# Exponent arguments from one stationary tile of 128 rows, with the hi and lo parts of both logarithms stacked

## The chip, the cores and the metric

The kernel runs on one core of one Trainium2 chip. Five engines work from queues of their own: TensorE (PE, matrix products into PSUM), VectorE (DVE), ScalarE (ACT, functions from tables), GpSimd (POOL) and SyncE (SP, which issues most of the transfers). The metric is the device time of one execution in microseconds.

## The reference

`x` is 2048 positions by 640 channels. A layer norm, scaled and shifted by vectors computed from a condition `c`, feeds a state space convolution; its output, gated, is added to `x`; a second norm feeds a gated feed-forward block of width 1728, which is added too.

```python
dt = exp(log_dt)[:, None]; logdA = dt * (A_re + 1j * A_im)
P = exp(logdA[:, :, None] * l[None, None, :])            # 640 x 128 x 2048
K = einsum("dn,dnl,dn->dl", Cc, P, dt * Bc).real          # one filter of 2048 taps a channel
y = irfft(rfft(u, 2L) * rfft(K, 2L))[:L] + u * Dskip      # causal convolution
out = (silu(h @ w1) * (h @ w3)) @ w2
```

The change concerns the filter `K` alone. The position is split as l = 64 a + b, with a below 32 and b below 64, so that the filter of a channel is a product of a slow table (over a) and a fast table (over b) summed over the 128 states n. A table entry is exp(decay) times a cosine or a sine. The magnitude of C B dt^2 goes into the slow table's exponent as half its logarithm squared.

## The kernel before, in words

Channels are worked in 40 steps of 16 (step k; 8 steps make one of five chunks of 128 channels). For each step:

- PA (`exp_fast`, lines 444 to 454) makes the fast exponents on PE, 128 states by 16 channels by 64 values of b, into a PSUM tile `pa`. XA (`fast`) takes their Exp on ACT into the table `A`.
- PQ (`exp_slow`, lines 455 to 465) and XQ (`slow`) do the same for 32 values of a, in `pq`.
- PH makes phases on POOL, in integers; AB, CO and SI (`absph`, `cosine`, `sine`, lines 496 to 507) turn them into a cosine and a sine on ACT.
- E1, E2, A1, A2 multiply exponentials and trigonometric tables on DVE; kg multiplies the tables on PE into the filter, K scales it on DVE, pt takes the first stage of its transform on PE, uk copies it out on ACT.

Ten steps behind, the convolution works on chunks already transformed: st (second stage of the transform, line 590), kc, T, Y (products), iv (inverse, line 632), zt (copy and store).

The exponents are products of a logarithm with a step length. TensorE rounds its fp32r operands, so each logarithm is split into a rounded part hi and the rest lo. `polar` (lines 237 to 291) makes both logarithms with states on the partitions: the decay `are * dt` in `lt[:, 0]` and the magnitude `q + ld` in `lt[:, 1]`. It turns them by PE with one transpose per chunk and logarithm (line 283), and splits what comes out on ACT (line 285, the rounded copy) and DVE (line 286, the difference). That gives four tiles `lah`, `lal`, `lmh`, `lml` with 128 channels of a chunk on the partitions, in four groups r of 32 rows. `polar` runs for chunk 0 in the head of the kernel, and for chunks 1 to 4 spread over the first loop.

The moving operands are `r2` (fast) and `r1` (slow): a 32 x 32 unit matrix (`selx`), each one multiplied by the step lengths (`stepx`), so that each of 32 rows yields its own channel's exponents. `sel`, half the unit matrix, adds half the magnitude. A half step (rr) is 8 channels in one group of 32 rows. Fast: two matmuls (hi and lo) for each of two half steps, 4. Slow: four (hi and lo of the decay on `r1`, hi and lo of the magnitude on `sel`) for each of two, 8. All of them use 32 rows of the array.

The order of work: the head and the first loop (`for tk in range(LAG)`) are ordered by the planner except what is marked to keep its order; ACT always keeps it. There, exponents are made for two steps at once (`exps`), in two PSUM buffers A and B, which `u_stage1` and `polar` use as well. Behind it come ten rounds of four steps, whose order is the list `ROUND` word by word (line 841): all engines keep it. In the rounds pa and pq have the single buffer B. In rounds 2 to 6 the rest of the conditioning vectors is computed in five late pieces, each called right behind a word of the list (lines 853 to 857): `late_load` (a transfer), `late_sums` (PE, line 299), `late_part` (DVE), `late_cols` (PE, lines 366 and 370), `late_out` (DVE). The feed-forward block stands behind the rounds, with its matmuls at lines 1059 to 1110 and 1258, all recorded at line 102.

Of the kernel before, what the change touches and what calls it, by code (L numbers as in the profile page):

```python
# [17 lines left out]
P = 128  # L18
L = 2048
D = 640  # L20
# [17 lines left out]
def consts():  # L38
# [32 lines left out]
    stepx = np.concatenate([np.arange(NB), 64 * np.arange(NA)])[None].repeat(P, 0)  # L71
# [36 lines left out]
def tile_kernel(ctx: ExitStack, tc: tile.TileContext, a):  # L108
# [50 lines left out]
    hp = kp.tile([P, 1], F32, name="hp")  # L159
    V.memset(hp, math.pi / 2)  # L160
# [13 lines left out]
    lah = once([P, KD, P], F32R, "lah")  # L174
    lal = once([P, KD, P], F32R, "lal")
    lmh = once([P, KD, P], F32R, "lmh")
    lml = once([P, KD, P], F32R, "lml")
    r2 = once([P, NA, NB], F32R, "r2")
    r1 = once([P, NA, NA], F32R, "r1")
    sel = once([P, NA], F32R, "sel")  # L180
# [5 lines left out]
    lt = pm_.tile([P, 2, D - DC], F32, name="lt")  # L186
# [50 lines left out]
    def polar(cs, E):  # L237
# [37 lines left out]
        rows = lambda v: v[:, :nk * P].rearrange("n (k r p j) -> n k r p j", k=nk, p=4, r=4)  # L275
        for k in range(nk):
            E.tensor_tensor(rows(lt[:, 0])[:, k], nat(are)[:, k], nat(dtc)[:, k], op=OP.mult)
        for k in range(nk):
            V.tensor_tensor(rows(lt[:, 1])[:, k], nat(q)[:, k], nat(ld)[:, k], op=OP.add)
        for i, (hi, lo) in enumerate(((lah, lal), (lmh, lml))):  # L280
            pT = psS.tile([P, 2, 512], F32, name="pT", tag="AB"[i], bufs=1)
            for k in range(nk):
                PE.transpose(pT[:, 0, k * P:(k + 1) * P], lt[:, i, k * P:(k + 1) * P], ident)
            pv = pT[:, 0, :nk * P].rearrange("p (k n) -> p k n", k=nk)
            acopy(hi[:, k0:k0 + nk], pv)
            V.tensor_tensor(lo[:, k0:k0 + nk], pv, hi[:, k0:k0 + nk].bitcast(F32), op=OP.subtract)
# [151 lines left out]
    def exp_rows(s):  # L438
        return s // SPC, slice((s % SPC) // 2 * 8, (s % SPC) // 2 * 8 + 8), [
            (rr, slice((2 * (s % 2) + rr) * 32, (2 * (s % 2) + rr) * 32 + 32)) for rr in range(2)]  # L440

    pA, pQ = {}, {}

    def exp_fast(steps):

        for s in steps:
            pA[s] = psS.tile([P, 2, 512], F32, name="pa", tag="AB"[s % 2] if not in_order[0] else "B", bufs=1)
        for w, st in ((lah, True), (lal, False)):
            for s in steps:
                ch, js, rows = exp_rows(s)  # L450
# [50 lines left out]
    def cosine(s):  # L501
        act(cs[s], cs[s], AF.Sin, scale=-2 * math.pi / TURN, bias=hp)
# [946 lines left out]
```

## Time and profile before

| | |
|---|---|
| median of 3 runs | 1009.01 us (1006.81 to 2960.16) |
| profiled execution | 1006.52 us, span 1004.4 us |
| granted TensorE clock, mean | 0.95 |
| busy: PE, DVE, ACT, POOL | 922.5, 730.2, 543.3, 349.5 us |
| line 452 (`pa`), PE busy | 33.6 us |
| line 464 (`pq`), PE busy | 29.4 us |

The page of the profile gives busy times of the whole span; views of the trace give groups of instructions by line, the chain of work that ended last, instructions in order of time (start, length, engine, operation, "output<-input", and in brackets the idle time before it with what ended it), and busy times by stretch. A row in order of time may merge neighbours of one kind (x2, x16). Busy times of PE overlap, since matmuls are pipelined.

### The profile page before, as it was taken

To read this page: it belongs to the slowest core of one execution; us is meant where nothing else is said; L and a number is where in the kernel's file an instruction comes from. 1 tells how busy PE (TensorE), PEld (TensorE's weight loads), DVE (VectorE), ACT (ScalarE), POOL (GpSimd) and SP (SyncE) were. 2 spreads that over 40 slices of the span, in tenths; PEclk is the share of its full clock that TensorE was granted. 3 is DMA by queue.
4 is the path that set the end of the run, shared out by engine and by line. 5 is a ranking of instruction groups with operands and counts; after the bars stand their busy time and mean duration, and the time that the engine had idled before them with its cause. 6 is when DMAs were issued, how large, how long until landed. Compare 5 with 4: busy or idle time off the path is not lost.

```text
span 1004.4 us, 20629 instructions
## 1 busy us (share of the span) xinstructions
PE 922.5 (92%) x8214; PEld 689.2 (69%) x8214; DVE 730.2 (73%) x1227; ACT 543.3 (54%) x793; POOL 349.5 (35%) x330
## 2 busy tenths in 40 slices
PE   5898779999989888789999999989989999999998
PEld 2535456666666666467888888766768888888786
DVE  4598887888888885677666675687696666676765
ACT  3658687988889953255433332344643333333332
POOL 1543353434444611314222233444342222224441
PEclk9855779999999999999999999999999999999999
DMA  9462393666665689592221213969231111123352
GB/s 268 170 234 80 135 237 106 160 179 181 189 174 139 182 211 265 183 278 77 70 61 55 56 37 104 254 204 282 86 128 56 54 53 53 53 81 103 92 199 76
DMA packets 103571, 140.74 MB, mean 140 GB/s; under 512 B 20564, under 2 KB 62676, under 8 KB 103476
## 3 DMA queue, kind: packets, MB, share of 16 engines
q1 hardware_dynamic: 92692, 113.60, 39.4%
q10 hardware_dynamic: 8480, 18.09, 6.1%
q0 software_dynamic: 2304, 7.74, 2.4%
q8 instruction: 64, 1.05, 0.4%
q14 instruction: 31, 0.25, 0.1%
HBM read 107.94 MB, written 31.46 MB: 139 GB/s over the span
## 4 chain that ended last, share of the span: by engine, by line
PE 62%; ACT 14%; DVE 10%; DMA 7%; issue 3%; POOL 3%; SPq 1%; ACTq 0%; DVEq 0%; POOLq 0%
PE ps L102 43%; PE p L590 4%; ACT cs L135 3%; ACT A L135 3%; PE pa L452 2%; ACT ph L135 2%; PE pz L632 2%; PE pk L541 2%; PE pq L464 2%; DMA zs<-zt 2%; DMA A<-zs 2%; ACT L135 2%; PE pt L559 1%; PE pu L426 1%; DMA rw<-in_w_dram 1%
## 5 line engine op out<-in xcount | busy, mean ns | idle before, releaser
L102 DVE TENSOR_TENSOR s<-ps,s 128x512 f32<-128x512 f32 x138 | 94.8, 688 | 77.0 <-PE ps L102 76.3
L492 POOL TENSOR_TENSOR ph<-thi,iota 128x1024 int32<-128x1024 int32 x40 | 85.4, 2135 | 170.2 <-DVE A L528 79.1
L102 DVE TENSOR_TENSOR gl<-rw,gh 128x640 fp32r<-128x640 f32 x87 | 84.2, 968 | 62.4 <-ACT gh L102 59.4
L102 ACT CAST gh<-rw 128x640 fp32r<-128x640 f32 x87 | 63.2, 727 | 115.4 <-PE ps L102 79.6
L102 POOL TENSOR_TENSOR rw<-rw,gbr 128x512 f32<-128x512 f32 x56 | 82.4, 1478 | 104.4 <-DMA rw<-in_w_dram 90.1
L102 POOL TENSOR_TENSOR S<-rw 128x256 f32<-128x256 f32 x46 | 35.7, 778 | 176.2 <-DVE S0l L102 159.1
L590 PE MATMUL p<-uk,s 128*64 128x256 f32 x640 | 79.2, 390 | 15.3 <-PE pa L452 5.6
L102 PE MATMUL ps<-xA,gh 128*128 128x512 f32 x280 | 89.0, 396 | 0.7 <-DVE h L102 0.4
L102 PE MATMUL ps<-gh,uh 128*128 128x512 f32 x224 | 89.3, 399 | 0.0
L102 PE MATMUL ps<-gl,uh 128*128 128x512 f32 x224 | 88.8, 397 | 0.0
L102 PE MATMUL ps<-gh,ul 128*128 128x512 f32 x208 | 82.5, 397 | 0.0
L590 PEld LDWEIGHTS p<-uk,s 128*64 128x64 f32 x640 | 45.2, 138 | 40.6 <-PE pa L452 8.4
L102 PEld LDWEIGHTS ps<-xA,gh 128*128 128x128 f32 x280 | 53.0, 191 | 14.0 <-ACT xA L102 0.9
L102 PE MATMUL ps<-xA,gl 128*128 128x512 f32 x140 | 55.3, 395 | 0.3 <-DVE gl L102 0.3
L135 ACT ACTIVATE A<-pa 128x1024 f32<-128x1024 f32 x40 | 40.4, 1024 | 25.4 <-PE pa L452 23.9
L517 DVE TENSOR_TENSOR E<-A,cs 128x1024 f32<-128x1024 f32 x40 | 52.3, 1307 | 2.5 <-ACT cs L135 1.8
L559 PE MATMUL pt<-s,K 128*64 128x128 f32 x640 | 48.7, 297 | 4.9 <-ACT uk L138 4.9
L524 DVE TENSOR_TENSOR A<-A,ph 128x1024 f32<-128x1024 f32 x40 | 50.3, 1256 | 0.0
L102 PEld LDWEIGHTS ps<-gl,uh 128*128 128x128 f32 x224 | 43.2, 193 | 9.5
L102 PEld LDWEIGHTS ps<-gh,uh 128*128 128x128 f32 x224 | 43.2, 193 | 9.1
L632 PEld LDWEIGHTS pz<-Y,i 64*128 64x128 f32 x640 | 38.5, 187 | 15.5 <-issue 13.1
L632 PE MATMUL pz<-Y,i 64*128 64x128 f32 x640 | 44.5, 283 | 4.5 <-issue 3.5
(244 smaller groups left out, 2366.7 us busy)
## 6 DMA issues: line engine op xcount, KB each, us to landing
rw<-in_w_dram ACTq DMA_DIRECT2D x44, 320.0 KB
us<-u SPq DMA_DIRECT2D x16, 640.0 KB
s<-in_s_dram SPq DMA_DIRECT2D x40, 256.0 KB
i<-in_i_dram SPq DMA_DIRECT2D x40, 256.0 KB
rw<-in_wg_dram SPq DMA_DIRECT2D x31, 320.0 KB
rw<-in_wu_dram SPq DMA_DIRECT2D x28, 320.0 KB
uk<-us SPq DMA_DIRECT2D x32, 256.0 KB
zs<-zt SPq DMA_DIRECT2D x32, 256.0 KB
```

The source lines that it names most:

```text
L102: ins = fn(*args, **kw)
L135: return tc.keep_in_program_order(S.activation(*args, **kw))
L426: PE.matmul(pu[h][hh * 64:hh * 64 + 64, q, :320], s1r[r], x[r, hh * 320:hh * 320 + 320], start=not (one and h == 0), stop=True, tile_posit ...
L452: keep(PE.matmul(pA[s][:, rr, :], w[r, ch, :], r2[r, js, :].rearrange("p j b -> p (j b)"), start=st, stop=not st, tile_position=(r.start, 0)))
L464: keep(PE.matmul(pQ[s][:, rr, :256], w[r, ch, :], rv, start=(i == 0), stop=(i == 3), tile_position=(r.start, 0)))
L492: hold(G.tensor_tensor(p, bc(thi[:, sl], 2, NPH), bc(iota, 1, SD), op=OP.mult))
L517: keep(V.tensor_tensor(EC[s][:, :, 1:3, :], AA[s][:, :, 1:3, :], mid(cs[s]), op=OP.mult))
L524: keep(V.tensor_tensor(A[:, :, 1:3, :], A[:, :, 1:3, :], mid(ph[s]), op=OP.mult))
L541: keep(PE.matmul(pk[dq * 32:dq * 32 + 32, g, :], x[:, g * 4 + dq, 1, :], x[:, g * 4 + dq, 0:3:2, :], start=(st == 0), stop=(st == 1), tile ...
L559: keep(PE.matmul(pt[c * 64:c * 64 + 64, g, :], kk[:, g, :], s1[:, c, :], start=True, stop=True, tile_position=(0, c * 64)))
L590: keep(PE.matmul(p2[par * 64:par * 64 + 64, pi, c, :], s2[:, pi * 2 + par, c * 64:c * 64 + 64], uk[:, 0:kn + 1:kn, f, :], start=True, stop ...
L632: ins = keep(PE.matmul(pz[:, par, (g % 2) * 2 + pi, :], i1[r, pi, c, :], Y[r, pi, c, :], start=(c == 0), stop=(c == 1), tile_position=(par ...
```

## The change

The four tiles become one, `lx`, with 128 rows for each group of 32 channels: 32 rows each of decay hi, magnitude hi, decay lo, magnitude lo. `polar` lays both logarithms side by side in `lt`, multiplies each such block by the unit matrix twice, into the upper and the lower 64 partitions of PSUM, rounds all of it, and replaces the lower half by the difference. The step lengths in `stepx` have the matching rows: for the magnitude 0 (fast) and 0.5 (slow). One matmul over 128 rows then yields a half step: 2 for the fast, 2 for the slow exponents of a step. `sel` goes. Beside that, the cosine's bias becomes a number in place of the tile `hp`, and the late pieces become words of the round (LS, LP, LC, LO), each standing one word earlier than it ran before; the load stands ahead of the round's first word.

```diff
-    stepx = np.concatenate([np.arange(NB), 64 * np.arange(NA)])[None].repeat(P, 0)
+    stepx = np.tile(np.concatenate([np.arange(NB), 64.0 * np.arange(NA)]), (4, NA, 1)).reshape(P, NB + NA)
+    stepx[P // 4:P // 2] = stepx[3 * P // 4:] = np.repeat((0, 0.5), (NB, NA))
...
-    lah = once([P, KD, P], F32R, "lah")
-    lal = once([P, KD, P], F32R, "lal")
-    lmh = once([P, KD, P], F32R, "lmh")
-    lml = once([P, KD, P], F32R, "lml")
+    lx = once([P, KD, 4, P], F32R, "lx")
...
-        for i, (hi, lo) in enumerate(((lah, lal), (lmh, lml))):
-            pT = psS.tile([P, 2, 512], F32, name="pT", tag="AB"[i], bufs=1)
-            for k in range(nk):
-                PE.transpose(pT[:, 0, k * P:(k + 1) * P], lt[:, i, k * P:(k + 1) * P], ident)
-            pv = pT[:, 0, :nk * P].rearrange("p (k n) -> p k n", k=nk)
-            acopy(hi[:, k0:k0 + nk], pv)
-            V.tensor_tensor(lo[:, k0:k0 + nk], pv, hi[:, k0:k0 + nk].bitcast(F32), op=OP.subtract)
+        low = slice(P // 2, P)
+        for k in range(0, nk, 2):
+            n = min(2, nk - k)
+            pT = psS.tile([P, 2, 512], F32, name="pT", tag="AB"[k // 2], bufs=1)
+            for i in range(n):
+                for r in range(4):
+                    for h in range(2):
+                        PE.matmul(pT[h * 64:h * 64 + 64, i, r * P:(r + 1) * P],
+                                  lt[:, k + i, r].rearrange("n i c -> n (i c)"), ident,
+                                  start=True, stop=True, tile_position=(0, h * 64))
+            to = lx[:, k0 + k:k0 + k + n].rearrange("p k r n -> p k (r n)")
+            acopy(to, pT[:, :n])
+            V.tensor_tensor(to[low], pT[low, :n], to[low].bitcast(F32), op=OP.subtract)
...
+    def exponents(to, steps, table, n):
+        for s in steps:
+            ps = to[s] = psS.tile([P, 2, 512], F32, name="pa", tag="AB"[s % 2] if not in_order[0] else "B", bufs=1)
+            js = slice((s % SPC) // 2 * 8, (s % SPC) // 2 * 8 + 8)
+            for rr in range(2):
+                keep(PE.matmul(ps[:, rr, :8 * n], lx[:, s // SPC, 2 * (s % 2) + rr, :],
+                               table[:, js, :].rearrange("p j b -> p (j b)"), start=True, stop=True))
...
-        act(cs[s], cs[s], AF.Sin, scale=-2 * math.pi / TURN, bias=hp)
+        act(cs[s], cs[s], AF.Sin, scale=-2 * math.pi / TURN, bias=math.pi / 2)
...
-        "PA+6 E2+3 pt+2 XA+6 A2+3 E2+4 kc+4 PQ+6 uk+2 PH+7 T+4 kg+3 XQ+6 AB+6 PA+7 K+3 iv+2 XA+7 AB+7 "
-        "Y+4 PQ+7 A1+4 st+5 XQ+7 A2+4 PH+8 kg+4 CO+5 iv+3 kc+5 K+4 CO+6 T+5 pt+3 zt+3 Y+5 uk+3 E1+5 "
+        "PA+6 E2+3 pt+2 XA+6 A2+3 E2+4 kc+4 PQ+6 uk+2 PH+7 T+4 kg+3 XQ+6 AB+6 LS+4 PA+7 K+3 iv+2 XA+7 "
+        "AB+7 LP+4 Y+4 PQ+7 A1+4 LC+4 st+5 XQ+7 LO+4 A2+4 PH+8 kg+4 CO+5 iv+3 kc+5 K+4 CO+6 T+5 pt+3 "
```

46 lines of the change are left out of this document (13 added, 33 removed), and 2 rows, old and new, of the table ROUND.

## The prediction

> **What bounds the kernel now.** I read the page's span first, then where the exponents stand (the view of line 452), then the table of busy time by stretch, since one mean covers very unlike stages.
>
> ```profile
> span 1004.4 us, 20629 instructions
> ...
> L452 PE MATMUL pa<-r,lal x80: 382/392/792, 24.1 to 348.5; 32*128 32x512 f32 x80
> ...
> core 0: us, PE busy (x) PEld busy (x) DVE busy (x) ACT busy (x) POOL busy (x), PEclk, DMA share, GB/s
> 100.00:135.00 35.00, 28.06 (x430) 15.93 (x426) 31.37 (x53) 24.23 (x30) 13.76 (x11) 0.68 0.41 154
> 195.00:225.00 30.00, 27.41 (x514) 19.78 (x510) 24.82 (x42) 26.34 (x33) 12.96 (x8) 1.00 0.64 175
> ```
>
> The last fast exponent starts at 348.5 us; no edit reaches behind that but four cosines, so the other 650 us only start earlier or later. Steps 0 to 3 lie in the head, 4 to 11 in the first loop (to 135 us, TensorE well under its full clock: granted 0.68), 12 to 39 in seven written-out rounds. In a round no engine is full: PE 27.4 of 30 us, ACT 26.3, DVE 24.8, and they wait for each other in turn. The ACT queue of a round shows where:
>
> ```profile
> 217.84 1.02 ACT L135 ACTIVATE A<-pa 128x1024 f32<-128x1024 f32 x1
> ...
> 232.44 0.60 ACT L135 ACTIVATE A<-pq 128x512 f32<-128x512 f32 x1 [1.19 <-PE pq L464]
> 233.06 1.28 ACT L135 ACT_TABLE_LOAD   x1
> ...
> 237.48 1.01 ACT L138 COPY zt<-pz 128x1024 f32<-128x1024 f32 x1 [0.46 <-PE pz L632]
> ...
> 239.95 1.14 ACT L135 ACTIVATE cs<-cs,hp 128x1024 f32<-128x1024 f32 x1
> 240.98 1.05 ACT L135 ACTIVATE ph<-ph 128x1024 f32<-128x1024 int32 x1
> 241.93 1.05 ACT L135 ACTIVATE cs<-ph 128x1024 f32<-128x1024 int32 x1
> ...
> 248.18 1.02 ACT L135 ACTIVATE A<-pa 128x1024 f32<-128x1024 f32 x1
> ...
> 251.70 1.02 ACT L135 ACTIVATE A<-pa 128x1024 f32<-128x1024 f32 x1 [1.08 <-PE pa L452]
> ```
>
> A round lasts 248.18 - 217.84 = 30.34 us. Its first half (Exp) is ping-pong: pa and pq share one PSUM buffer, so ACT waits for PE (1.08 and 1.19 us in these rows) and PE for ACT. Its second half (Sin, from the table load at 233.06) has ACT back to back but for 0.46 us.
>
> **The fast exponents (pa).** Four matmuls become two. In PE's queue:
>
> ```profile
> 249.25 0.39 PE L464 MATMUL pq<-r,lah 32*128 32x256 f32 x2 [0.58 <-ACT A L135]
> 249.48 0.28 PE L464 MATMUL pq<-r,lal 32*128 32x256 f32 x2
> 249.60 0.27 PE L464 MATMUL pq<-sel,lmh 32*128 32x256 f32 x2
> ...
> 249.91 1.09 PE L559 MATMUL pt<-s,K 128*64 128x128 f32 x16
> ...
> 255.30 0.50 PE L452 MATMUL pa<-r,lah 32*128 32x512 f32 x2
> 255.64 0.39 PE L452 MATMUL pa<-r,lal 32*128 32x512 f32 x2
> 255.96 0.88 PE L559 MATMUL pt<-s,K 128*64 128x128 f32 x12
> ...
> 132.51 0.57 PE L452 MATMUL pa<-r,lah 32*128 32x512 f32 x4
> 132.92 0.39 PE L452 MATMUL pa<-r,lal 32*128 32x512 f32 x4
> ...
> 467.18 141.99 PE ps L102 x625
> ```
>
> The two of a pair sit in different groups of 32 rows and run side by side: a pair takes 255.64 - 255.30 = 0.34 and then 0.32 us, and at 132.51 four of them take 0.41. So four instructions are two passes of 512 columns, and the new two are also two passes. A full-array pass is priced by the MLP: 141.99 / 625 = 0.227 us. Two of them with the weight load before the first (0.34 - 0.227 = 0.11) take 0.57 to 0.66 us against 0.66. I take nothing, and keep 0.21 (2 x 0.227 against 0.66) as the other end. The Trainium skill, "TensorE: Matmul & The Clock Gate", Part 3, says this of the form removed: a matmul on 32 rows lasts as long as one on 128, the gain being that several run at once; the trace agrees (0.41 us for four). The Trainium skill's same page, "Back-to-back issue gap", gives about 131 ns for a 512-column matmul in a stream, by which two would cost 0.26 us, an estimate; the 0.227 us here speaks against it, and the sum does not use it.
>
> **The slow exponents (pq).** Here eight become two: 249.91 - 249.25 = 0.66 us for four pairs, the first 0.23, the second 0.12, the last two 0.31 with the change of shape behind them. Two passes go, at 0.12: 0.24 us a step, both in PE's time and in ACT's wait. Ends: 0 (the two that stay lose their side-by-side loads) and 0.43 (all but the first).
>
> **The cosine's bias.** A number takes the place of a tile.
>
> ```profile
> L135 ACT ACTIVATE cs<-cs,hp 128x1024 f32<-128x1024 f32 x40 | 46.0, 1149 | 0.4
> ...
> L135 ACT ACTIVATE ph<-ph 128x1024 f32<-128x1024 int32 x40 | 41.4, 1050 | 0.0
> ```
>
> Sine, which has no such tile, is 99 ns shorter; in the queue above, starts lie 1.03 us apart behind a cosine and 0.95 behind a sine. I take 0.09 us each, 0.36 a round (0 if the number is put into a tile after all).
>
> **The late pieces moved** (rounds 2 to 6). LS now stands ahead of PA+7, LC ahead of st+5, LP ahead of Y+4, LO ahead of A2+4; the load of xw is issued ahead of E1+2 in place of behind it, and since E1+2 issues no DMA, SP's queue keeps its order; POOL has no part in any of it.
>
> ```profile
> 229.18 1.48 PE L299 MATMUL pm<-xw,sc 128*32 128x384 f32 x10
> ...
> 234.48 0.83 PE L366 MATMUL pm<-one,xw 128*128 128x1 f32 x6
> ...
> 231.79 0.42 DVE L614 TENSOR_TENSOR Y<-T,p 128x256 f32<-128x256 f32 x1 [2.51 <-PE pz L632]
> ```
>
> LP falls into the 2.51 us in which DVE waits ahead of Y. LO is a new wait of DVE ahead of A2+4: it waits for LC, behind it are A2+4 and then kg+4 on PE; since A1+4 (1.2 us) stands before it, I cost it at nothing, and at LC's 0.83 if A1+4 were not there.
>
> **One round walked through**, counted from its first Exp at 217.84. PQ+4 and PQ+5 stand between two works of the ring and give 0.24 each: PA+6 comes 0.48 earlier, kg+3 behind PQ+6 0.72. Now LS (1.48, of which 1.41 to the start of the next) comes ahead of PA+7: XA+7 is 1.41 - 0.72 = 0.69 *later* than now. It had room: iv+2, behind both in either order, is 0.72 earlier, and PQ+7, which waited for iv+2, now waits for XA+7. Behind XA+7 ACT has AB+7 to do, so the last Exp and the table load come some 0.5 earlier, at 14.7 in place of 233.06 - 217.84 = 15.22. LC (0.83) no longer stands between st+5 and kg+4, and st+5 comes 0.2 earlier: kg+4 and iv+3 are 1.0 earlier, and so is the copy zt for which ACT waits. From there ACT is full; two cosines behind zt add 0.18. Sum: 1.2 us a round, five times 6.0. Rounds 7 and 8 have no late pieces; 0.72 and the cosines' 0.18 make 0.9 each, 1.8. The cosines of rounds 0, 1 and 9 give some 0.7. **Rounds: -8.5 us**, with -4.5 as one end (pq gives half on the ring) and -13 as the other (rival A). What is late next is the same ring, with ACT's Sin half as its tightest part.
>
> **What is added: the stacked weights.** Two transposes a chunk become eight fp32 matmuls, each recorded as two: 64 for the late four chunks, 16 for chunk 0.
>
> ```profile
> 106.75 1.06 PE pT L283 x4
> ...
> 107.83 0.59 ACT lmh L138
> ...
> 108.45 0.69 DVE lml L286
> ...
> 92.73 1.98 PE L559 MATMUL pt<-s,K 128*64 128x128 f32 x16
> ...
> 32.64 2.39 PE pr L323 x10
> ```
>
> pt has the new shape (128x64 weights, 128 columns): 1.98 / 16 = 0.12 us at the low clock, 0.068 (1.09 / 16, above) at full. 64 of them take 4.4 to 7.9 us against some 2.1 for the eight transposes (four in 1.06). ACT's copies double from 512 to 1024 columns (0.59 to 1.01, as zt), +0.84; DVE's subtraction on half the partitions is as long as its columns, about 0.69 to 1.22 (L517 below), +1.06. All in series, at the low clock, would be +7.7. DVE and PE have other work to put between, and PE stands idle soon after (stretches of PE alone; then an operation of DVE, two pieces of the chain, and pa's own time in the head):
>
> ```profile
> 110.00:115.00 5.00, 3.95 (x123) 1.00 0.01 3
> 115.00:120.00 5.00, 1.35 (x26) 0.90 0.65 264
> 120.00:125.00 5.00, 4.42 (x54) 0.50 0.00 0
> ...
> 104.21 1.22 DVE L517 TENSOR_TENSOR E<-A,cs 128x1024 f32<-128x1024 f32 x1
> ...
> 86.46 2.15 PE pq L464 x12
> ...
> 20.00:32.00 12.00, 3.85 (x8) 1.34 (x8) 1.00 0.98 302
> ```
>
> With PE busy for 1.35 us of the five from 115, 3.65 us can swallow about half; I take +3, with 0 and +7.7 as ends. Steps 4 to 11 give back: pq at the low clock, 2.15 us for two steps, loses half its passes, about 0.4 a step with what each costs beside them; where two steps run four wide, as pa at 132.51, the passes stay and nothing goes. Over eight steps I take 0.21 each, half of it: -1.7. Their pa gives nothing, and four wide it loses 0.2, inside the rounding. Cosines on the path, half of twelve: -0.5. **First loop: +0.8.** Head (the matmuls wait for both logarithms now, the first transpose for one; PE has the sums of w_mod to do meanwhile): 16 at 0.12 to 0.24 (2.39 / 10) = 1.9 to 3.8, less two transposes at 0.27 (1.06 / 4): about +2.2. PE bounds the head, but there pa stands in single pieces, 3.85 us busy for 8; half of them go, and with pq's share I take -1.6 of at most -1.9. **Head: +0.6.** The memset and the table sel that go are 0.2 us of a DVE that waits for a load.
>
> **Sum:** -8.5 + 0.8 + 0.6 = -7.1. The profiled execution took 1006.52 us, 2.1 around its span and 0.25% under the median of 1009.01: 1006.5 - 7.1 = 999.4, so **999.5 us**, 0.7% faster. A measurement of this kernel tells about 2% from no change.
>
> **Rivals.** *A, fast exponents gain as well* (0.23): if full-array passes take 0.227 with their loads hidden, the three of a round that stand on the ring give 0.21 each, 0.6 a round, 4.4 in seven: 995. For it the MLP's pitch; against it the weight load that PE can't begin before ACT frees the buffer.
> *B, slower than before* (0.17): the preparation holds both PSUM buffers A and B, which u_stage1 needs too, for half of its 64 matmuls, a copy and a subtraction each (4.0 + 1.0 + 1.2 = 6.2 us in place of 1.1 + 0.6 + 0.7 = 2.4). With nothing to put between, the whole +7.7 is on the path, and the gap it tears into PE puts the clock down, as the idle stretch from 115 does now (granted 0.50 from 120): up to half of the next 10 us, 5. Then -8.5 + (7.7 + 5 - 2.2) + 0.6 = +2.6: 1009. It decides once preparation costs the loop more than 10 us; for it speaks that DVE is busy 31 of 35 us there, against it the idle PE.
> *C, a warmer clock* (0.12): the clock, 0.50 at 120, is granted at 1.00 in the stretch from 110, behind the transposes and some dense pk. Sixty-four dense matmuls could raise it sooner and, filling the gap, hold it: of the 4.42 us of PE work in 120 to 125, and as much again behind it, up to half goes: 995. The Trainium skill, "TensorE: Matmul & The Clock Gate", Part 4, says that transposes don't count as activity for the clock as matmuls do, which would favour this; no row separates it.
> *D, rounds give nothing* (0.13): LS ahead of PA+7 takes from ACT what pq gave, and only the cosines remain (0.36 x 9 = 3): 1006.5 - 3 + 1.4 = 1005.
> Forecast 0.35 at 999.5. **Range 990 to 1010.** Faster by over 2% (below 986.4) needs A, C and a free preparation at once: 0.04; slower by over 2%: 0.03; within: 0.93.
>
> **What would show it.** Two pa from start to the next work 0.6 to 0.66 us, two pq about 0.42; cosines at 1050 ns; a round of 29.1 us with late pieces and 0.9 below now's without; XA+7 with an idle time of over 1 us ahead of it; 80 preparation matmuls of 7 to 11 us in all; the MLP unchanged in length. A pa of 0.45 would break the step on row groups; a round of 28 us or less the walk; a longer or colder stretch from 100 to 145 the price of the preparation.

## The result, and the profile after

The changed kernel took 994.09 us (median; 991.63 to 996.63) where the kernel before took 1009.43 on the same chip: ratio 0.9864, 95% interval 0.9839 to 0.9888. A second comparison gave 997.38 against 1006.07: 0.9921, interval 0.9894 to 0.9947. So it is 0.8 to 1.4% faster, within the 2% that a measurement of this kernel tells. The ratios are of fast executions alone; one of the kernel before took 2960.16 us and counts in the median of 1009.43 only. The forecast was 999.5, the range 990 to 1010.

The time is cut below at marks that both kernels have in ACT's queue: the load of the table of Sin at the end of the head, the first Exp of step 12 (the first written-out round), and the last copy zt.

| stretch, us | before | changed | difference | predicted |
|---|---|---|---|---|
| head, to the table of Sin | 43.87 | 35.28 | -8.59 | +0.6 |
| first loop, to the Exp of step 12 | 113.31 | 118.72 | +5.41 | +0.8 |
| rounds, to the last zt | 254.84 | 246.49 | -8.35 | -8.5 |
| what is left (loads, MLP) | 592.38 | 589.31 | -3.07 | 0 |
| span | 1004.40 | 989.80 | -14.60 | -7.1 |

(A part of the forecast's -8.5 for the rounds, some cosines of rounds 0 and 1, lies ahead of the Exp of step 12 and so in the loop's row.) The rounds came out as forecast to 0.2 us. The head and the loop did not, in opposite directions, and it is these two that the experiments are about.

A round first. From ACT's queue of the changed kernel (start, us, engine, line, operation, the wait ahead of it in brackets), the round that begins at 211.60:

```profile
211.60 1.02 ACT L136 ACTIVATE A<-pa 128x1024 f32<-128x1024 f32 x1
...
223.65 1.02 ACT L136 ACTIVATE A<-pa 128x1024 f32<-128x1024 f32 x1 [1.16 <-PE pa L447]
...
226.13 1.28 ACT L136 ACT_TABLE_LOAD   x1
...
229.84 1.01 ACT L139 COPY zt<-pz 128x1024 f32<-128x1024 f32 x1
...
240.36 1.02 ACT L136 ACTIVATE A<-pa 128x1024 f32<-128x1024 f32 x1
```

The round lasts 28.76 us in place of 30.34. Its last fast Exp waits 1.16 us for LS, as the walk had it, and starts 12.05 behind the first where it started 11.44 behind. The table is loaded at 14.53 (before 15.22, forecast 14.7). The copy zt waits no more (0.46 before), and the cosines take 1.06 in place of 1.15. So 0.69 comes from the Exp half and 0.89 from the Sin half. TensorE's queue in the same round:

```profile
212.68 0.51 PE L447 MATMUL pa<-r,lx 128*128 128x256 f32 x2 [0.35 <-ACT A L136]
213.12 1.09 PE L548 MATMUL pt<-s,K 128*64 128x128 f32 x16
214.14 0.73 PE L447 MATMUL pa<-r,lx 128*128 128x512 f32 x2
214.80 0.32 PE L530 MATMUL pk<-E 128*32 128x64 f32 x8
...
221.50 1.45 PE L300 MATMUL pm<-xw,sc 128*32 128x384 f32 x10
222.88 0.73 PE L447 MATMUL pa<-r,lx 128*128 128x512 f32 x2
```

LS is the row at 221.50, ahead of the last fast exponents. The two fast matmuls take 0.66 us to the start of the next work (214.14 to 214.80), exactly what the four took: four on 32 rows side by side were two passes, and two on 128 rows are two passes. The pair for the slow exponents takes 0.44 where the eight took 0.66.

Now the head. Instructions in order of time: ten matmuls of TensorE that sum a piece of w_mod, such tens again later, and ACT's table load that ends the head; first the kernel before, then the changed one:

```profile
16.41 1.92 PE L299 MATMUL pm<-uk,sc 128*32 128x256 f32 x10 [0.25 <-DVE cols L310]
25.82 1.91 PE L299 MATMUL pm<-A,sc 128*32 128x256 f32 x10
...
43.87 1.28 ACT L135 ACT_TABLE_LOAD   x1
```

```profile
13.03 1.98 PE L282 MATMUL pT<-ident,lt 128*64 128x128 f32 x16
16.82 1.05 PE L300 MATMUL pm<-uk,sc 128*32 128x256 f32 x10 [0.25 <-DVE cols L311]
22.13 1.05 PE L300 MATMUL pm<-A,sc 128*32 128x256 f32 x10
...
35.28 1.28 ACT L136 ACT_TABLE_LOAD   x1
```

Ten such matmuls take 1.9 us in the one trace up to 28 us, and 1.05 in the other from 16 us on. The preparation was priced there in the order of its cost (1.98 us for 16, forecast 1.9 to 3.8); what was not priced is that TensorE's clock is up behind it. The column of the granted clock does not show this here: it reads 1.00 in the slice from 15 to 22 us of both, as it does in every trace until the clock falls for the first time. Behind that it agrees with the lengths. In a second trace of the changed kernel ten such matmuls take 1.91 us at 24.36 and twenty take 1.91 at 38.35, and the clock (third number from the end) reads:

```profile
24.40:26.20 1.80, 1.80 (x11) 0.51 (x11) 0.56 (x2) 0.44 (x1) 0.00 (x0) 0.50 0.97 312
38.40:40.20 1.80, 1.80 (x23) 0.81 (x20) 1.80 (x5) 1.78 (x4) 1.25 (x2) 1.00 0.00 0
```

So the length of these matmuls tells the clock: 1.9 us for ten at 0.50 ("down"), 0.95 to 1.05 at 1.00 ("up").

The first loop, by the stretch from the end of the Exps of steps 4 to 7 to the table for steps 8 to 11, in the table of busy times (PE, PEld, DVE, ACT, POOL, then clock and DMA); before, then changed:

```profile
89.25:125.76 36.51, 26.55 (x418) 14.42 (x414) 30.59 (x58) 28.37 (x34) 14.78 (x13) 0.69 0.30 121
```

```profile
81.21:121.37 40.16, 30.04 (x460) 19.16 (x452) 33.88 (x62) 28.96 (x35) 15.58 (x14) 0.63 0.28 108
```

Two groups of the changed kernel's work in that stretch (busy time and mean of one, then idle time ahead), the matmuls and the subtractions of the preparation:

```profile
L282 PE MATMUL pT<-ident,lt 128*64 128x128 f32 x64 | 5.8, 365 | 0.0
...
L287 DVE TENSOR_TENSOR lx<-pT,lx 64x1024 fp32r<-64x1024 f32 x2 | 2.5, 1228 | 0.8 <-ACT lx L139 0.8
```

This stretch is 3.65 us longer, and the preparation in it was the suspect.

### The profile page after: what moved, and what is told of

It is laid out like the page before. It is cut to its first block, busy times and chain, and to the rows that moved or that the text cites. A ratio compares the mean times of both kernels' runs of the same rounds, so it can differ in the third digit from the quotient of the medians.

```text
span 989.8 us, 20130 instructions
## 1 busy us (share of the span) xinstructions
PE 904.1 (91%) x7964; PEld 679.0 (69%) x7964; DVE 734.0 (74%) x1224; ACT 539.9 (55%) x792; POOL 348.5 (35%) x330
## 3 DMA queue, kind: packets, MB, share of 16 engines
q0 software_dynamic: 2304, 7.74, 2.3%
## 4 chain that ended last, share of the span: by engine, by line
PE 42%; DVE 5%; DMA 3%; ACT 2%; POOL 2%; issue 2%; SPq 1%; DVEq 0%; ACTq 0%; POOLq 0%
PE ps L103 42%; DMA A<-zs 2%; DVE ul L103 1%; DVE T L103 1%; DVE xm L103 1%; DMA rw<-in_w_dram 1%; DVE gl L103 1%; ACT s L103 1%; ACT gh L103 1%; DMA xm<-in_x_dram 1%; SPq L103 1%; DVE s L103 1%; POOL s L103 0%; POOL S L103 0%; DVE h L103 0%
## 5 line engine op out<-in xcount | busy, mean ns | idle before, releaser
L136 ACT ACTIVATE A<-pa 128x1024 f32<-128x1024 f32 (+1 forms) x80 | 64.3, 813 | 27.1 <-PE pa L447 25.0
L447 PE MATMUL pa<-r,lx 128*128 128x512 f32 (+1 forms) x160 | 52.1, 415 | 10.7 <-ACT A L136 5.6
L513 DVE TENSOR_TENSOR A<-A,ph 128x1024 f32<-128x1024 f32 x40 | 52.6, 1315 | 0.0
L506 DVE TENSOR_TENSOR E<-A,cs 128x1024 f32<-128x1024 f32 x40 | 50.2, 1254 | 0.7 <-ACT cs L136 0.7
L447 PEld LDWEIGHTS pa<-r,lx 128*128 128x128 f32 x160 | 25.8, 203 | 34.5 <-ACT A L136 18.2
L530 PE MATMUL pk<-E 128*32 128x64 f32 x1280 | 46.4, 236 | 3.4 <-DVE E L509 3.4
```

The costliest lines, as they stand in the source:

```text
L136: return tc.keep_in_program_order(S.activation(*args, **kw))
L447: keep(PE.matmul(ps[:, rr, :8 * n], lx[:, s // SPC, 2 * (s % 2) + rr, :], table[:, js, :].rearrange("p j b -> p (j b)"), start=True, stop= ...
L506: keep(V.tensor_tensor(EC[s][:, :, 1:3, :], AA[s][:, :, 1:3, :], mid(cs[s]), op=OP.mult))
L513: keep(V.tensor_tensor(A[:, :, 1:3, :], A[:, :, 1:3, :], mid(ph[s]), op=OP.mult))
L530: keep(PE.matmul(pk[dq * 32:dq * 32 + 32, g, :], x[:, g * 4 + dq, 1, :], x[:, g * 4 + dq, 0:3:2, :], start=(st == 0), stop=(st == 1), tile ...
```

## The experiments

Each is a kernel of its own, measured against the kernel before on the same chip.

**The late order undone.** The round's words as they were, the pieces called behind a word again; stacked weights and bias stay.

```diff
-        "... AB+6 LS+4 PA+7 K+3 iv+2 XA+7 AB+7 LP+4 Y+4 PQ+7 A1+4 LC+4 st+5 XQ+7 LO+4 A2+4 ..."
+        "... AB+6 PA+7 K+3 iv+2 XA+7 AB+7 Y+4 PQ+7 A1+4 st+5 XQ+7 A2+4 ..."
```

> The changed kernel with the late pieces back at their old places (called behind PA+7, Y+4, st+5, A2+4, the load behind E1+2). Theory: the new order is part of what the rounds gained, because LC stands in front of st+5 where PE waits and no longer between st+5 and kg+4; without it the copy zt waits for PE again, the five rounds with late pieces go from 28.75 to about 29.35 us, the sum is +3 us, and rounds 7 and 8 do not change. Rival: the order is worth nothing (my walk of the round gave it 0.15 us): these rounds stay at 28.7 to 28.9 us. Second rival: LS ahead of PA+7 costs, and the rounds come down to 28.2.

Measured: ratio 0.9958 (0.9936 to 0.9981). The rounds with late pieces last 29.49 us:

```profile
214.34 1.02 ACT L136 ACTIVATE A<-pa 128x1024 f32<-128x1024 f32 x1
...
226.74 1.06 ACT L136 ACTIVATE cs<-ph 128x1024 f32<-128x1024 int32 x1 [0.58 <-POOL ph L482]
228.06 0.60 ACT L136 ACTIVATE A<-pa 128x512 f32<-128x512 f32 x1 [0.26 <-PE pa L447]
...
233.32 1.01 ACT L139 COPY zt<-pz 128x1024 f32<-128x1024 f32 x1 [0.86 <-PE pz L621]
...
243.83 1.02 ACT L136 ACTIVATE A<-pa 128x1024 f32<-128x1024 f32 x1
```

So the order is worth 0.73 us a round. Three waits of ACT, 1.70 us in all, stand here that the new order takes away, for the one of 1.16 behind LS. A reading by which the order is worth nothing falls.

**The bias undone.** The tile `hp` is back.

```diff
-        act(cs[s], cs[s], AF.Sin, scale=-2 * math.pi / TURN, bias=math.pi / 2)
+        act(cs[s], cs[s], AF.Sin, scale=-2 * math.pi / TURN, bias=hp)
```

> The changed kernel with the cosine's bias read from a tile again. Theory: the second half of a round is ACT back to back, so 0.09 us come back for each of four cosines: rounds of 29.1 us in place of 28.75, +3 to +3.6 us over all ten rounds, head and loop within 0.5 us. Rival: the 96 ns are hidden by the waits of the ring, and the rounds stay within 0.1 us.

Measured: ratio 0.9953 (0.9930 to 0.9976); rounds of 28.96 us (216.46 to 245.42), 0.2 more than in the changed kernel. That is the worth of two cosines and not of four. The rows say where the other two went: behind zt stands the copy uk, which needs pt of TensorE. It starts 19.28 us behind the round's first Exp with the tile (235.74) and 19.27 with the number (230.87, as pt ends at 229.73 + 1.09 = 230.82). What the first two cosines save is waited away there; only the two behind it shorten the round.

**Only the stacked weights.** Both of these undone.

> The changed kernel with the late pieces back in their old places and the cosine's bias back in a tile: only the stacked weights are left of the change. If the parts add up: rounds with late pieces of 29.49 + 0.21 = 29.7 us (30.34 before), the head, the preparation and steps 4 to 11 as in the changed kernel, and 1004 to 1005 us in all, ratio 0.996 to 0.998. If the late order only pays once the ring is shorter, or the bias pays more where ACT is fuller, the round comes out further from 29.7 than 0.1.

Measured: 1007.58 us, ratio 1.0019 (1.0003 to 1.0035). The round lasts 29.67 us (216.70 to 246.37), the sum of the parts to 0.03: of the 1.58 us that a round gained, 0.67 come from the stacked weights, 0.18 from the bias, 0.73 from the order. In all, the change that gives this case its name brings no gain: what it wins in the rounds (3.0 us from step 12 to the last zt, 251.83 against 254.84) the loop takes back. The total was missed: 1004 to 1005 had been expected. Of the 10.2 us between this kernel and the changed one on the same chip (997.38) the rounds give 5.1; the rest stays open.

**Half of the preparation's matmuls.** Each block is multiplied by the unit matrix once, into the upper 64 partitions, and the difference is taken from these.

```diff
-                    for h in range(2):
+                    for h in range(1):
...
-            acopy(to, pT[:, :n])
-            V.tensor_tensor(to[low], pT[low, :n], to[low].bitcast(F32), op=OP.subtract)
+            acopy(to[:64], pT[:64, :n])
+            V.tensor_tensor(to[low], pT[:64, :n], to[:64].bitcast(F32), op=OP.subtract)
```

> The changed kernel with half of the preparation matmuls: PSUM's upper 64 partitions only, and the difference read from there and written to the lower rows of lx. Same result, 32 matmuls in place of 64 in the loop and 8 in place of 16 in the head. Theory on the loop: the preparation stands on its path, so the stretch from the Sin table load at 86 us to the Exp table load at 121 us shortens by 1.5 to 3 us. On the head there are two theories: if the new matmuls raise the clock because they keep PE busy for 2 us, half of them may not do it, and the head goes back by up to 8 us (whole 994 to 1000); if being matmuls and not transposes is enough, the head stays within 1 us of 35.3 (whole 990 to 993). Rival on the loop: hidden, no change.

Measured: ratio 0.9928 (0.9899 to 0.9957), and the preparation of chunks 1 to 4 in TensorE's queue:

```profile
103.25 5.41 PE L282 MATMUL pT<-ident,lt 128*64 128x128 f32 x32
```

Half as many take 5.41 us in place of 5.78, at a mean granted clock of 0.67 and 0.63: the two halves of a block stood in different groups of columns and ran side by side. The stretch of the loop lasts 40.46 us (40.16), so nothing is gained, where 1.5 to 3 had been expected. The prediction's price, 4.4 to 7.9 us for 64, was that of pt, whose matmuls alternate between the halves of the columns as well; the 5.78 lie inside it. The head's table comes at 41.51, which the first theory of the head would explain; what follows on the clock takes that away.

**Transposes in place of the late matmuls.** Chunks 1 to 4 by eight transposes of 128x128, with two copies and two subtractions of 64 partitions for each buffer (the expectation says sixteen transposes; four chunks of two make eight).

```diff
+                    for q in range(2):
+                        PE.transpose(pT[:, i, q * P:(q + 1) * P],
+                                     lt[:, k + i, 2 * q:2 * q + 2].rearrange("n r i c -> n (r i c)"), ident)
+                for e in range(2):
+                    half = lx[:, k0 + k:k0 + k + n, e::2]
+                    got = pT[e * 64:e * 64 + 64, :n, :2 * P].rearrange("p k (r n) -> p k r n", r=2)
+                    acopy(half[top], got)
+                    V.tensor_tensor(half[low], got, half[top].bitcast(F32), op=OP.subtract)
```

> Chunks 1 to 4 are prepared by 16 transposes of 128x128 (two slices of 32 rows and both logarithms at once, as many elements as the 64 recorded matmuls give) in place of the 64; the high parts leave by two copies of 64 partitions and the low parts by two subtractions for each buffer. Chunk 0 keeps its 16 matmuls. Theory, the matmuls of the preparation hold ACT up: from the end of the exponentials of steps 4 to 7 to the next Exp table (40.2 us, 36.5 before) it takes 37 to 38.5, since 16 transposes at 0.27 take 4.3 less the part beside other work, and the first buffer is free after 2.1 in place of 3.7; the total is 2 us under the changed kernel's. Rival, DVE and ACT set the stretch, whose copies and subtractions become no shorter (0.59 x 4 for 1.01 x 2): 40 or more, and the total equal.

Measured: 998.59 us, ratio 0.9940 (0.9918 to 0.9963). The stretch lasts 39.59 us: 0.6 to 1.0 less than in the two traces of the changed kernel, where the theory had asked for 37 to 38.5. That does not clear TensorE's matmuls. The eight transposes take 1.97 us, but with four copies and four subtractions in place of two and two the last subtraction starts 8.32 us behind the last logarithm, where it started 6.93 behind it.

**The split ahead of the transposes** (and 26 matmuls at the start, of which below). High and low parts are made before they are turned, so DVE has one subtraction of 128x1024 in place of two of 64x1024.

```diff
+            st = lx[:, k0:].rearrange("n k r (h c) -> n k r h c", h=2)
+            acopy(st[:, :, :, 0], lt.rearrange("n k r i c -> n k r (i c)"))
+            V.tensor_tensor(st[:, :, :, 1], lt..., st[:, :, :, 0].bitcast(F32), op=OP.subtract)
...
+                        PE.transpose(pT[:, i, r * P:(r + 1) * P], st[:, k + i, r]..., ident)
+                acopy(lx[:, k0 + k:k0 + k + 2].rearrange("p k r n -> p k (r n)"), pT)
```

> As the changed kernel with the 26 matmuls, and chunks 1 to 4 are split into high and low parts before they are transposed: one copy of 1024 columns on ACT and one subtraction of 1024 on DVE (1.2 us) in place of two, then 16 transposes of 128x128 and two copies. Theory, DVE, busy for 34 of the 40 us from the exponentials of steps 4 to 7 to the next Exp table, sets that stretch: 1.2 us of work and 0.8 to 1.3 of waits go, 38 to 39 in place of 40.2 to 40.6. Rival, the path from ACT through the transposes and back sets it, with a copy more on it: 40 or more. The total differs from that of the kernel with the 26 matmuls alone by no more than this.

Measured: 994.85 us, ratio 0.9880 (0.9845 to 0.9914), a little under the changed kernel's second comparison but not apart from it. It is apart from the kernel with the same 26 matmuls and no split, 1002.44 on the same chip (0.9944, 0.9921 to 0.9966): 7.6 us, where no more than the stretch's gain had been expected. The two traces show 3.3 of them (spans of 997.9 and 1001.2), spread over head, loop, rounds and rest; the cause stays open. The stretch, by the table of busy times:

```profile
87.06:126.36 39.30, 32.53 (x432) 18.61 (x428) 31.77 (x62) 29.91 (x35) 16.11 (x14) 0.59 0.28 112
```

DVE has 2.1 us less to do than in the changed kernel (31.77 against 33.88) and the stretch is shorter by 0.9; against the kernel that has the same 26 matmuls and no split (39.50, DVE busy 33.87) by 0.2. So DVE's total doesn't set it either. None of the three edits shortens the stretch by more than 1.0. The queues themselves, the kernel before and then the changed one, with the last of the logarithms (`lt`), ACT's first copy and DVE's second subtraction:

```profile
102.26 0.16 DVE L401 SCALAR_TENSOR_TENSOR rs<-mv,rs 128x2 f32<-128x2 f32 x1 [0.86 <-POOL rs L400]
102.34 0.28 DVE L279 TENSOR_TENSOR lt<-uk 128x128 f32<-128x128 f32 x1
106.43 0.59 ACT L138 CAST lah<-pT 128x512 fp32r<-128x512 f32 x1 [0.81 <-PE pT L283]
108.45 0.69 DVE L286 TENSOR_TENSOR lml<-pT,lmh 128x512 fp32r<-128x512 f32 x1 [0.71 <-ACT lmh L138]
```

```profile
82.69 0.88 DVE L398 BATCH_NORM_STATS2 st<-x 128x6 f32<-128x320 f32 x2
83.59 0.44 DVE L398 BATCH_NORM_STATS2 st<-x 128x6 f32<-128x320 f32 x1
96.67 0.16 DVE L402 SCALAR_TENSOR_TENSOR rs<-mv,rs 128x2 f32<-128x2 f32 x1 [0.86 <-POOL rs L401]
96.75 0.28 DVE L274 TENSOR_TENSOR lt<-uk 128x128 f32<-128x128 f32 x1
100.81 1.01 ACT L139 CAST lx<-pT 128x1024 fp32r<-128x1024 f32 x1 [2.21 <-PE pT L282]
103.96 1.23 DVE L287 TENSOR_TENSOR lx<-pT,lx 64x1024 fp32r<-64x1024 f32 x1 [0.16 <-ACT lx L139]
```

Counted from the start of the stretch, the operation ahead of the last logarithm comes at 13.01 us before (102.26 - 89.25) and at 15.46 in the changed kernel (96.67 - 81.21), 2.45 later, and the changed kernel's matmuls start only when that logarithm is done (at 97.08). The three statistics of x in the second fence (1.3 us) stand at the head of the stretch; in the kernel before they were done ahead of it, beside the Exps of steps 4 to 7:

```profile
86.70 0.49 DVE L397 BATCH_NORM_STATS2 st<-x 128x6 f32<-128x320 f32 x1
87.42 0.88 DVE L397 BATCH_NORM_STATS2 st<-x 128x6 f32<-128x320 f32 x2
88.32 0.44 DVE L397 BATCH_NORM_STATS2 st<-x 128x6 f32<-128x320 f32 x1
```

These Exps are 1.34 us shorter in the changed kernel (8.55 against 9.89; 8.54 or 8.55 in all ten traces with stacked weights, 8.93 to 9.89 in the four without), so a part of what they gave was work moved behind them. Taken together, the Exps of steps 4 to 7 and the stretch last 48.71 us for 46.40. Counted from the start of these Exps, the last logarithm is done 1.1 later (24.37 for 23.26), by the order that the planner found; the second subtraction starts 6.93 behind it for 5.83; what follows takes 17.41 for 17.31. So about half of the 2.3 arises ahead of the preparation and half in it. The half in it is less DVE's longer subtractions than ACT's waits for the matmuls ahead of its two copies (2.21 and 1.09, before 0.81 twice): in six traces with the sixty-four matmuls these take some 4.9 to 6.3 us by the clock, and the subtraction starts 6.28 to 7.74 behind the logarithm. That is read from the rows; no run put the old order back.

**TensorE's clock in the head.** First, eight such matmuls (recorded as sixteen) beside the transposes of chunk 0 in the kernel *before*, their output unused:

```diff
+            if k0 == 0:
+                for r in range(4):
+                    PE.matmul(pT[:64, 1, r * P:(r + 1) * P], lt[:, i, :64], ident, start=True, stop=True, tile_position=(0, 0))
```

> The kernel before, with eight fp32 matmuls of 128 columns (64 weights wide) added beside the two transposes of chunk 0 in the head; their results are not used. Theory: what the head of the changed kernel gained, 8.6 us up to the Sin table load (43.87 to 35.28), is TensorE's clock, raised at about 15 us by the new matmuls, and not the fewer exponent matmuls: here the sums of w_mod behind them then take 1.05 us for ten in place of 1.92, the table load comes at 36 to 38 us, and the whole is 3 to 7 us faster than before. Rival: the gain lay in the exponents and in the order; then the head stays at 44 us or later by the 1 to 2 us that the added matmuls take, and the whole is 0 to 2 us slower than before.

Measured: ratio 0.9963 (0.9939 to 0.9986). The ten of w_mod fall to 1.05 us by 20.97, so the clock does rise, but the table of Sin comes at 42.47: by 28.5 the clock is down again. The 0.4% come in this trace from the loop (108.96 us for 113.31), which neither theory had; that stays open. Second, the reverse: the changed kernel with transposes for chunk 0 too, its sixteen matmuls gone.

> As the kernel before it, and chunk 0 too is prepared by transposes, two of 128x128 as in the kernel before the change, in place of 16 recorded matmuls. Theory, the 16 matmuls raise TensorE's clock in the head: without them the ten matmuls of a piece of w_mod take 1.9 us at 16.8 in place of 1.05, and the table of Sin is loaded at 40 to 44 us in place of 35.3 to 37.4; the total 3 to 5 us over the kernel with transposes for chunks 1 to 4 alone, if nothing swallows it. Rival 1, the full-array exponents raise it: the matmuls go from 1.9 to 1.05 only behind the first of these, at 20 to 23 us, and the table comes at 37 to 39. Rival 2, the clock has nothing to do with either and the head is shorter by its exponents alone: 35 to 37.

Measured: 1001.44 us, ratio 0.9953 (0.9935 to 0.9971); ten matmuls take 1.9 us up to 28 us and the table is loaded at 42.32. So far the sixteen matmuls look like the cause. Then came the traces that don't fit. The kernel with transposes for chunks 1 to 4 *keeps* the sixteen in the head, and its clock stays down:

```profile
13.31 1.97 PE L294 MATMUL pT<-ident,lt 128*64 128x128 f32 x16 [0.21 <-DVE lt L274]
17.49 1.92 PE L311 MATMUL pm<-uk,sc 128*32 128x256 f32 x10 [0.25 <-DVE cols L322]
...
44.19 1.28 ACT L136 ACT_TABLE_LOAD   x1
```

**Both kernels once more**, with nothing edited.

> The changed kernel once more, beside three others on one chip. The kernel whose late order alone is undone took 1003.45 us and the one whose bias alone is undone 1003.32, each 0.46% under the kernel before; by their traces the parts are worth 0.7 and 0.2 us a round, some 4 and 1.5 us in all. Theory 1, the gain of 1.4% of the first comparison holds: ratio 0.985 to 0.988. Theory 2, a good part of it is scatter of the head and of the loads: the changed kernel lies only as far under those two as their parts are worth, 999 to 1002, ratio 0.990 to 0.994. In both, five rounds of 28.75 us with late pieces; and by theory 1 the Sin table of the head is loaded at 35 us, by theory 2 anywhere between 35 and 38.

> The kernel before once more, for a second trace of its head. If its narrow tiles (32 rows or 32 columns of weights) and two transposes never raise TensorE's clock, ten matmuls of a piece of w_mod take 1.9 us from 10 to 30 us again and the Sin table is loaded at 43 to 45 us. If the clock is a draw of each execution, whatever the kernel, they take 1.05 in a part of the head and the table comes at 36 to 42.

Measured: the changed kernel at the ratio 0.9921 told above, which lies with its theory 2. Its ten matmuls take 1.05 us at 16.48 but 1.91 again at 24.36, and the table is loaded at 40.18, later than either theory allowed. The kernel before has, this time:

```profile
15.82 1.05 PE L299 MATMUL pm<-uk,sc 128*32 128x256 f32 x10 [0.25 <-DVE cols L310]
23.24 1.91 PE L299 MATMUL pm<-A,sc 128*32 128x256 f32 x10
...
40.92 1.28 ACT L135 ACT_TABLE_LOAD   x1
```

So the clock of the head differs from one execution of a program to the next, in both kernels. The sixteen matmuls are neither needed for it (here) nor enough (above).

**A clock raised before the head begins.** 26 matmuls on ones in the first 10 us, in which TensorE waits for loads, in the changed kernel and in the kernel before.

```diff
+    hot, pw = pm_.tile([P, 512], mybir.dt.bfloat16, name="hot"), psS.tile([P, 2, 512], F32, name="pw", tag="A", bufs=1)
+    warm = [V.memset(hot, 1.0)] + [tc.keep_in_program_order(PE.matmul(pw[:, 0], hot[:, :P], hot, start=True, stop=True)) for _ in range(26)]
```

> The changed kernel with 26 bf16 matmuls of 128x128 weights and 512 columns of ones in the first 10 us, in which TensorE waits for the first loads. Theory, the head is ruled by when TensorE's clock rises and falls: the first ten matmuls of w_mod take 1.05 in place of 1.89 us and the Sin table comes at 33 to 36 (35.3 and 40.2 in the two traces of the changed kernel); 2 to 4 us less in all, ratio 0.985 to 0.99 where the changed kernel had 0.992, with less scatter. Rival, the head's work can't hold the clock: it is back at 1.9 us for ten before 20 us, the table comes at 37 to 42, and the total is that of the changed kernel.

> The kernel before with the same 26 matmuls in the first 10 us. By the theory its head gains too, the Sin table at 38 to 41 in place of 43.9, 2 to 5 us in all, ratio 0.995 to 0.998; so part of the difference of the two heads was clock and no exponents. By the rival, that its tiles of 32 rows or columns don't hold the clock, ten matmuls of w_mod are back at 1.9 us from 15 on and the table comes at 42 to 44, ratio 1.000.

Measured: 0.9944 (0.9921 to 0.9966) and 1.0001 (0.9977 to 1.0024). TensorE's queue of the first:

```profile
1.70 7.53 PE L189 MATMUL pw<-hot 128*128 128x512 bf16 x26 [1.70 <-DVE hot L189]
10.14 1.02 PE L300 MATMUL pm<-uk,sc 128*32 128x256 f32 x10 [0.91 <-DMA uk<-in_w_mod_dram]
24.93 1.91 PE L300 MATMUL pm<-A,sc 128*32 128x256 f32 x10
...
41.38 1.28 ACT L136 ACT_TABLE_LOAD   x1
```

The clock is up from the first matmul of the head and down again by 19 us; the table comes at 41.38 (42.44 in the kernel before so treated). The rival held in both: the head did not keep the clock, and raising it sooner bought nothing. That it can keep it, other traces show (up from 15 to 17 us until 29 to 34, below). All traces side by side, in us; "clock up" is where the granted clock reads 1.00 or, ahead of its first fall, where ten matmuls of w_mod or others of known length run at the short time:

| kernel | clock up in the head | head | loop | rounds | rest |
|---|---|---|---|---|---|
| before | 37 to 41 | 43.87 | 113.31 | 254.84 | 592.38 |
| before, again | 13 to 20, 34 to 37 | 40.92 | 113.46 | 254.70 | 595.42 |
| before, 26 matmuls | 10 to 18, 35 to 38 | 42.44 | 113.82 | 256.44 | 591.40 |
| before, 8 matmuls | 17 to 28 | 42.47 | 108.96 | 255.04 | 594.03 |
| changed | 16 to 33 | 35.28 | 118.72 | 246.49 | 589.31 |
| changed, again | 14 to 20, from 34 | 40.18 | 120.84 | 246.74 | 594.44 |
| only stacked weights | 17 to 34 | 35.91 | 121.02 | 251.83 | 590.54 |
| late order undone | 15 to 29, from 32 | 37.30 | 117.37 | 251.13 | 592.80 |
| bias undone | 15 to 29, from 32 | 37.39 | 120.29 | 249.28 | 594.64 |
| half preparation | 15 to 21 | 41.51 | 119.62 | 247.85 | 593.62 |
| changed, 26 matmuls | 10 to 19, from 36 | 41.38 | 117.33 | 247.42 | 595.07 |
| 26 matmuls, split | 10 to 19, 36 to 39 | 41.13 | 116.89 | 246.71 | 593.17 |
| transposes, late chunks | from 43 | 44.19 | 118.22 | 247.47 | 594.02 |
| transposes, all | from 37 | 42.32 | 117.72 | 248.52 | 593.64 |

At like clock the heads hardly differ: 40.18 against 40.92 where it is up from 13 or 14 to 20 and from 34, 44.19 against 43.87 where it is down to 37 or longer. Counted from 10 us to the end of the head, the clock is down for 8 to 9 us in the four heads of 35.3 to 37.4, for 17 to 25 in the seven of 40.2 to 42.5, and for 27 to 33 in the other three, of 42.3 to 44.2; where both kernels occur in a group, they hardly part. The loop's excess is no scatter: 109.0 to 113.8 us in the four traces without stacked weights, 116.9 to 121.0 in the ten with them. The five kernels with the changed head and preparation (changed, again, only stacked weights, and the two undone) take on average 37.2 for the head and 119.6 for the loop; the two traces of the kernel before 42.4 and 113.4. The head's -5.2, which is the clock's draw in these few traces, and the loop's +6.3 about cancel, and the rounds' 8 remain: 8.7 us is what the medians of the second comparison differ by. The rest, 589 to 595 in both kernels alike, accounts for 3 of the first pair's 14.6.

## Why the prediction was right in its sum and wrong in two terms

That both medians, 994.09 and 997.38, lie in the range is in part luck: what the loop cost beyond the forecast was made up by heads that happened to have a warm clock, and the misses inside the rounds cancel.

**The fast exponents give nothing: right.** 0.66 us for two passes, before and after. Rival A, which had them gain 0.21 each, falls with that row. (What the prediction takes from the Trainium skill, "TensorE: Matmul & The Clock Gate", on the length of a matmul on 32 rows stands there in the section "Why this matters for your kernels", not in Part 3.)

**The slow exponents give 0.24 a step: right.** 0.22 in TensorE's queue; 0.67 a round where three of them on the ring were counted at 0.72.

**The bias gives 0.09 a cosine: right**, and in a round two of the four pay, as the walk had it. 1059 ns on average in the group over the whole kernel:

```profile
L136 ACT ACTIVATE cs<-cs 128x1024 f32<-128x1024 f32 x40 | 42.4, 1059 | 0.4
```

**A round with late pieces gains 1.2: right in mechanism, small by 0.38.** The walk had XA+7 0.69 later (0.61 measured), the table at 14.7 (14.53), and zt's wait of 0.46 gone (it is). By the runs with parts undone, pq gave 0.67 (0.72 forecast) and the cosines 0.18 to 0.21 (0.18); the term that was mis-sized is the order, 1.2 - 0.72 - 0.18 = 0.3 in the forecast, 0.73 in the run. LO, costed at nothing as a new wait of DVE, shows none in the round. Rival D, the order taking back what pq gave, is refuted by the run with the order undone: the order itself gave 0.73.

**Rounds 7 and 8 gain 0.9 each: wrong.** Round 7 goes from 28.44 to 28.02 us, and what follows, from the first Exp of round 8 to the last zt, from 74.57 to 74.42. In ACT's queue of the changed kernel a wait stands there that the kernel before does not have:

```profile
310.44 1.06 ACT L136 ACTIVATE cs<-ph 128x1024 f32<-128x1024 int32 x1 [0.58 <-POOL ph L482]
```

Before, ACT waited twice 0.34 us for pq; now it waits 0.58 for POOL's phases, which take back most. POOL was not among the things that the walk had late next. In five rounds the walk was short by 1.8, in the later ones long by about as much: the total of -8.35 is close to -8.5 partly because these two misses cancel.

**The first loop costs 0.8: wrong, it costs 5 to 7.** The step that failed is "steps 4 to 11 give back". The first four gave 1.34 us, a part of it work moved out; the next four cost 1.67 (10.96 to 12.63) where they were to give. ACT's and TensorE's queues of the changed kernel:

```profile
125.09 1.02 ACT L136 ACTIVATE A<-pa 128x1024 f32<-128x1024 f32 x1 [1.41 <-PE pa L447]
128.52 0.60 ACT L136 ACTIVATE A<-pa 128x512 f32<-128x512 f32 x1 [2.40 <-PE pa L447]
...
125.78 1.98 PE L548 MATMUL pt<-s,K 128*64 128x128 f32 x16
```

and ACT's of the kernel before:

```profile
131.17 1.08 ACT L135 ACTIVATE A<-pq 128x512 f32<-128x512 f32 x2 [2.18 <-PE pq L464]
```

All sixteen pt stand ahead of the slow exponents, for which ACT waits 2.40 us; before, six did, and ten behind, and ACT waited 2.18. The largest new wait is the 1.41 ahead of the second fast Exp. All its waits in these Exps come to 4.65 us (1.41, 2.40, 0.17, 0.67) for 2.85 (2.18, 0.35, 0.32). Four matmuls of fast exponents at once take 1.13 us to the next work (129.52 to 130.65) for 0.73 before (132.51 to 133.24): they lose 0.4, where the prediction knew of 0.2 and rounded it away. And 1.89 us more pass from the table of Sin to the Exps of step 4 (37.38 against 35.49), which the prediction had not looked at; in the other traces with stacked weights these are 36.0 to 37.5, in those without 32.2 to 36.9, so a part of it may be scatter. The preparation was priced at +3; the rows give it some 1.1 in this pair, and 0.5 to 1.9 over the six traces. The prediction took the order outside the rounds as given; the change altered it.

**The head costs 0.6: near at like clock (-0.7, +0.3, and -1.1 with the 26 matmuls), and no help.** What the forecast lacked is that the head's time ranges from 35 to 44 us with TensorE's clock, by the execution. Rival C looked to the clock, but to 105 to 125 us and to the new matmuls as its cause. In its place the clock was no warmer (0.63 over the stretch of the loop, before 0.69), and in the head the sixteen matmuls are not shown to raise it; that it had named 995 is luck. Rival B, the preparation tearing a gap that puts the clock down, saw that the loop would cost far more, but 10.5 us is above the 5 to 7 measured, and the gap's part in it was not tested; the rounds outweighed it.

**What stays open.** Whether the stacked head has its clock up more often than the old one: of the traces without the 26 matmuls, seven of eight heads with such matmuls had it up by 17 us, and one of three without them, which is too few. Why the kernel before with eight added matmuls has a loop 4 us shorter, and why the split kernel is 7.6 us faster than the one without the split. And why the medians of the two comparisons lie 0.6% apart.

The Trainium skill, "TensorE: Matmul & The Clock Gate", Part 1, says that the window by which the clock is raised runs freely, so one and the same kernel warms up at another instruction each time. The traces agree: with the same sixteen matmuls the clock was up at 14, 15, 16 and 17 us, and once not before 43. The same part calls the cost of that ramp under 1% of a usual span; here the heads of all traces lie within 9 us of 1000, which agrees, and yet is about the size of everything the change brought.

## What to carry to other kernels

Count passes, not instructions: small matmuls side by side in the array are already one pass, and folding them into a full one saves only what ran one behind the other. Where a planner sets the order, an edit is also a new order: compare the order of each queue in the stretches that the edit never names, before pricing the edit's own operations there. And before a difference of a head of 40 us is explained, look at the same ten matmuls in several executions: if they take 1.05 us in one and 1.9 in the next, the difference may be the clock's.

## What the runs showed of the hardware

Two matmuls of 64 columns of weights in different halves of the columns run side by side as well as those in different rows: 64 took 5.78 us and 32 of one half 5.41 (granted clock 0.63 and 0.67); at the low clock of the head, 16 of both halves took 1.98 us in the changed kernel and 8 of one half 1.97 in the kernel before with added matmuls. TensorE's clock stayed down through 20 us of nearly unbroken work in one trace of the kernel before (16.41 to 36.5, ten matmuls of 128x32 weights and 256 columns in 1.92 us), and in three kernels of three it had been raised by 10 us and was down again by 19. Which of the work holds it is not shown: with the same instructions it was up to 20 us in one trace of the changed kernel and to 33 in the other. And the granted clock of the profile reads 1.00 ahead of its first fall, over matmuls of both lengths; from that fall on, it goes with them (0.50 and 1.00).
